# Two steps of a weight rounding and a one-row subtraction, moved from VectorE to GpSimd in a gated linear-attention and maxout-FFN kernel

## The chip, the cores and the metric

The kernel runs on one NeuronCore of a Trainium2 chip. The metric is the device time of one launch in microseconds (us). Three runs of the kernel before took 585.05, 585.9 and 587.58 us; the median is 585.9 us. Engine names in the profile: PE is TensorE (PEld its weight loads), DVE is VectorE, ACT is ScalarE, POOL is GpSimd, SP is SyncE, which issues the DMAs.

## The reference

Two stages are computed. The first is a recurrence over 768 steps, for 4 batches of 8 heads with head size 48. A complex gate turns and shrinks a state, and a real output is read from it:

```
mag = sqrt(a_re^2 + a_im^2);  scale = min(mag, 0.999) / (mag + 1e-6)
for t: S = (a_re + i a_im) * scale * S + k[t] v[t]^T      (complex S, real part read)
       y[t] = q[t] . Re(S)
```

The second is a feed-forward block on y, laid out as 3072 tokens by 384 features:

```
h = max(x @ w1, x @ w2, x @ w3)        # 384 -> 768
out = h @ w_out                        # 768 -> 384
```

The four weight matrices arrive as 64-bit floats, and the chip's matrix engine wants 32-bit ones. So the kernel turns each pair of 32-bit words into one float32 by work on bits: this is the part that the change touches.

## The kernel before, in words

**Tiling.** The tokens are cut into 12 groups (g = 0 to 11), each of 128 steps of two batches; the two batches of a group are called x and y. For each group the kernel loads a, k, q and v, works out the logarithm of the gate's size and its angle (the *turns*), sums them along the steps with matmuls, builds scaled and turned k and q, forms scores in blocks, carries a state from group to group, and puts the result through the feed-forward block. All float32.

**Order.** The order of the work is written out by hand. The string `SCHEDULE` is a list of steps (lines 21 to 130); `Wb0:0` is step b of weight block 0, `carry:1` the carry of group 1, `g0x:0` the first copy of scores of batch x in group 0. `program` walks the list once and each step issues its instructions. The class `Bound` (line 191) ties each instruction to the one before on the same engine, so that every engine executes its own instructions strictly in the order of the list. An engine that waits for one step holds up every later step of its own.

**Weights.** The four matrices make 12 blocks (`weight_blocks`, line 373), each 128 partitions by 768 float32 at the end. They are taken in the order 0, 3, 6, 9, 10, 11, 1, 2, 4, 5, 7, 8. Block i is loaded by `WLi` and then goes through `weight_step` (line 399):

- a (ACT): the absolute value of the upper word, read as a float, to the scratch `ex`;
- b (DVE before): limits to it, `max` with 2^-15 and `min` with `LAST`, one tensor_scalar, in place in `ex`;
- c (DVE): a shift of `ex` to the left by 3 bits;
- d (ACT): the lower word, scaled to a few bits, as a float in the block's own place `dst`;
- e (DVE before): the integer sum of `ex` and the bits of `dst`, in `ex`;
- f (DVE): the sign of the upper word joined to `ex`, into `dst`;
- g (DVE, some blocks): a difference of blocks, for the maximum.

b needs a, c needs b, e needs c and d, f needs e. The scratch `ex` lies in the tile `xhx`, which has two places for it; blocks take them in turn (`EX`, line 133), so that step a of a block needs step f of the block two before it. In the profile `ex` is named xhx, and `dst` is w or wo. The program gives step e on DVE to a custom instruction on 1536 halfwords, shown as CUSTOM_DVE_ANT_0 xhx<-w,xhx.

**The carry.** Step `carry` (line 538) subtracts from row 0 of the tile `ai` the turns that the group before ended with: one partition by 768 elements, for 10 of the 12 groups. Ahead of it ACT writes `ai` (`cpai`); behind it `addi` on DVE reads `ai`, or, in groups 0 and 1, the matmuls of `cs` do.

**GpSimd.** Before the change POOL has little to do: the constants of `constants_early` (line 278), the masks of `constants_late` (line 309, step `CL:0` of the list), which end with zeros in the two score tiles `atm`, and three memsets (`Z3`, `Z4`, `Z2`, line 928). The masks and the zeros are needed by `g0x:0` (line 722), a DVE copy of scores under the mask `maskd` into `atm`. Since the masks depend on nothing but POOL's own work, POOL makes them at 8.4 to 16.8 us, far ahead of `CL:0`'s place in the list.

Of the kernel before, what the change touches and what calls it, by code (L numbers as in the profile page):

```python
# [11 lines left out]
FP = mybir.dt.float32  # L12
U8 = mybir.dt.uint8
I32 = mybir.dt.int32
U32 = mybir.dt.uint32
AF = mybir.ActivationFunctionType
OP = mybir.AluOpType
# [119 lines left out]
def kernel(  # L137
# [36 lines left out]
    LAST = float(np.array(0x47EFFFFF, dtype=np.int32).view(np.float32))  # L174
# [13 lines left out]
    T = {}  # L188
# [18 lines left out]
    pe, dve, act, pool, sp = (Bound(e) for e in (nc.tensor, nc.vector, nc.scalar, nc.gpsimd, nc.sync))  # L207
    mm = pe.matmul

    def banks(nm, n=None):  # L210

        ps = psum.tile([P, 2, 512], FP, tag="ps", name=nm)
        T["ps"] = ps
        return ps if n is None else ps.rearrange("p a n -> p (a n)")[:, 0:n]
# [4 lines left out]
    def activation(func, **kw):  # L219

        need = SETS.get(func, T.get("set"))
        if need != T.get("set"):
            act.preload_act_table_set(need)
            T["set"] = need
        act.activation(func=func, **kw)

    def once(key, make):

        if key not in T:
            T[key] = make()  # L230
        return T[key]
# [167 lines left out]
    def weight_step(i, step):  # L399

        dst, src = blocks[i]
        n, m = dst.shape[1:]
        raw = T["raw", i].rearrange("p n (m w) -> p n m w", w=2)
        low, high = raw[:, :, :, 0].bitcast(U32), raw[:, :, :, 1]
        ex = xhx[:, 0:KD] if i in EX else xhx[:, KD + KF:]
        ex = ex.rearrange("p f t -> p (f t)").rearrange("p (n m) -> p n m", n=n).bitcast(I32)
        if step == "a":
            activation(out=ex.bitcast(FP), in_=high.bitcast(FP), func=AF.Abs)
        elif step == "b":
            dve.tensor_scalar(out=ex.bitcast(FP), in0=ex.bitcast(FP), scalar1=2.0 ** -15, scalar2=LAST,  # L410
                              op0=OP.max, op1=OP.min)
        elif step == "c":
            dve.tensor_single_scalar(out=ex, in_=ex, scalar=3, op=OP.logical_shift_left)
        elif step == "d":
            activation(out=dst, in_=low, func=AF.Copy, scale=2.0 ** -51, bias=2.0)
        elif step == "e":
            dve.tensor_tensor(out=ex, in0=ex, in1=dst.bitcast(I32), op=OP.add)
        elif step == "f":
            dve.scalar_tensor_tensor(out=dst.bitcast(I32), in0=high, scalar=-0x80000000, in1=ex,
                                     op0=OP.bitwise_and, op1=OP.bitwise_or)  # L420
        else:
            dve.tensor_tensor(out=dst, in0=dst, in1=blocks[i - i % 3][0], op=OP.subtract)
# [23 lines left out]
    def flat(t):  # L446
        return t.rearrange("p c h d -> p (c h d)")
# [22 lines left out]
    def gates(g, cs, name):  # L470

        if name not in names.split():
            return False
        lo, hi = cs[0] * DM, (cs[-1] + 1) * DM
        for nm in "Lwe":
            once((nm, g), lambda: nat1.tile([P, W], FP, tag=nm, name=nm))

        def part(nm):
            t = T[nm, g]
            return (flat(t) if len(t.shape) == 4 else t)[:, lo:hi]  # L480

        def flat_(nm):
            return T[nm, g]

        def of(t):
            return t.rearrange("p (c n) -> p c n", n=DM) if g < SUMS else t

        def total():
            return T["pw", g, lo][:, 0:len(cs), 0:DM] if g < SUMS else w

        L, w, e, ar, ai = (part(nm) if (nm, g) in T else None for nm in ("L", "w", "e", "ar", "ai"))
        if name == "sqr":
            activation(out=e, in_=ar, func=AF.Square)
        elif name == "sqi":
            activation(out=L, in_=ai, func=AF.Square)
        elif name == "add":
            dve._custom_dve(dve_ops.TENSOR_ADD_SAT, out=L, in0=L, in1=e, s0=LARGE, s1=SMALL)
        elif name == "lnL":
            activation(out=L, in_=L, func=AF.Ln)
        elif name == "expw":  # L500
            activation(out=w, in_=L, func=AF.Exp, scale=0.5)
        elif name == "expe":
            activation(out=e, in_=L, func=AF.Exp, scale=-0.5)
        elif name == "lne":
            activation(out=e, in_=e, func=AF.Ln, scale=1e-6, bias=1.0)
        elif name == "relu":
            activation(out=L, in_=L, func=AF.Relu, scale=-0.5, bias=lnmax)
        elif name == "Lnop":
            once(("Ln", g), lambda: nat2.tile([P, W], FP, tag="Ln", name="Ln"))
            dve.scalar_tensor_tensor(out=part("Ln"), in0=L, scalar=-LNMAX, in1=e, op0=OP.add, op1=OP.add)  # L510
        elif name == "abs":
            activation(out=e, in_=ar, func=AF.Abs)
        elif name == "pw":
            if g < SUMS:
                ps = T["pw", g, lo] = banks("pw")
                for n, c in enumerate(cs):
                    for i, t in enumerate(("w", "e")):
                        mm(out=ps[:, n, 0:DM], lhsT=ident, rhs=flat_(t)[:, c * DM:(c + 1) * DM], start=i == 0, stop=i == 1)
        elif name == "addw":
            if g >= SUMS:  # L520
                dve.tensor_tensor(out=w, in0=w, in1=e, op=OP.add)
        elif name == "lnw":
            activation(out=of(L), in_=total(), func=AF.Ln)
        elif name == "expL":
            activation(out=L, in_=L, func=AF.Exp, scale=-1.0)
        elif name == "mulai":
            dve.tensor_tensor(out=ai, in0=ai, in1=L, op=OP.mult)
        elif name == "mulw":
            dve.tensor_tensor(out=of(w), in0=total(), in1=of(L), op=OP.mult)
        elif name == "stt":  # L530
            dve.scalar_tensor_tensor(out=w, in0=w, scalar=2.0, in1=ai, op0=OP.subtract, op1=OP.mult)
        elif name == "sign":
            activation(out=ar, in_=ar, func=AF.Sign, bias=tiny)
        elif name == "cpai":
            activation(out=ai, in_=ar, func=AF.Copy, scale=-0.25, bias=0.25)
        elif name == "cpar":
            activation(out=ar, in_=ar, func=AF.Copy, scale=-1.0 / math.pi)
        elif name == "carry":
            if g % NS > 0:
                dve.tensor_tensor(out=ai[0:1], in0=ai[0:1], in1=T["carry", g], op=OP.subtract)  # L540
        elif name == "atan":
            activation(out=w, in_=w, func=AF.Arctan)
        elif name == "mulr":
            dve.tensor_tensor(out=w, in0=w, in1=ar, op=OP.mult)
        elif name == "addi":
            if g >= SUMS:
                dve.tensor_tensor(out=w, in0=w, in1=ai, op=OP.add)
        return True
# [372 lines left out]
    def run(name, g):  # L921
# [12 lines left out]
        elif name[0] in "TtMm" and name[1:].isdigit():  # L934
            product(name[0], int(name[1:]))
        elif name[0] == "W":
            i = int(name[2:])
            weight_load(i) if name[1] == "L" else weight_step(i, name[1])
        elif name[0] in "Uu" and name[1:].isdigit():
            up(g, int(name[1]), int(name[2]), name[0])  # L940
        elif name[0] in "Uu" and name[1:3].isdigit():
            up_one(2 * g + "xy".index(name[3]), int(name[1]), int(name[2]), name[0])
        elif name in SEVEN or name in ("ox", "oy") and g > 0:
            seven(g, name)
        elif name[0] == "J":
            join(name[1])
        elif name[-1] in "01" and gates(g, [int(name[-1])], name[:-1]):
            pass
        elif gates(g, list(range(C)), name):
            pass  # L950
        else:
            c = "xy".index(name[-1])
            x, name = g * C + c, name[:-1]
            if name in ("Lr", "Li"):
                load_a(g, c, *(("ar", a_re) if name == "Lr" else ("ai", a_im)))
            elif name in ("Lk", "Lq"):
                load_kq(g, c, *(("k", k) if name == "Lk" else ("q", q)))
            elif name == "Lv":
                load_v(g, c)
            else:  # L960
                assert angles(g, c, name) or turns(g, c, name) or factors(x, name) or scores(x, name) \
                    or state(x, name) or outputs(x, name) or project(x, name), name
# [45 lines left out]
```

## Time and profile before

| what | value |
|---|---|
| median of three runs | 585.9 us (585.05 to 587.58) |
| span of the profiled execution, first to last instruction | 585.0 us |
| mean granted TensorE clock | 0.980 |
| PE busy | 537.6 us, 92% of the span |
| DVE busy | 506.0 us, 86% |
| ACT busy | 439.4 us, 75% |
| POOL busy | 15.5 us, 3% |

A row of the profile by groups reads: engine, operation, what is written <- what is read, shapes, x count | busy us, mean ns of one | idle time of the engine just before. A row of the timeline reads: start in us from the span's start, duration in us, engine, line, operation; in brackets, the engine's idle time ahead of it and what ended it. Nearly all instructions carry line 200, the recording helper in `Bound`, so they are told apart by operation and tile. Two DVE instructions that follow each other overlap by about 0.08 us: the 128x768 ones last 0.95 us, and start 0.87 us apart when nothing holds them; the 128x768 tensor_scalars last 0.56 us and take a slot of 0.47 us.

### The profile page before, as it was taken

The page shows a single profiled execution, that of the slowest core. Times are in us where ns is not written, and L with a number is a line of the kernel's source. Part 1 is how long each engine was busy: PE and PEld are TensorE (multiplying, and loading weights), DVE is VectorE, ACT ScalarE, POOL GpSimd, SP SyncE. Part 2 cuts the span into 40 slices and gives each one's busy share as a digit, 9 for nine tenths or more (in the row PEclk, how much of TensorE's full clock was granted, in tenths as well). Part 3 has the DMA queues.
Part 4 walks back from the last instruction along what each step waited for, and adds up shares of the span by engine and source line. Part 5 has one row for each costly group of instructions (what it writes and reads, how often), then busy time and mean ns, then how long its engine had stood idle before and what let it go on. Part 6 is the DMA issues. An engine that isn't in the chain of part 4 may idle for free.

```text
span 585.0 us, 22777 instructions
## 1 busy us (share of the span) xinstructions
PE 537.6 (92%) x10118; PEld 454.6 (78%) x10118; DVE 506.0 (86%) x784; ACT 439.4 (75%) x740; POOL 15.5 (3%) x50
## 2 busy tenths in 40 slices
PE   2649979898999999999999999999999999999897
PEld 0336668767888888888898888898887888888886
DVE  5999999979898999999889889989998999877504
ACT  7999999857788778788788987887896797643110
POOL 8100100000000000000000000000000000000000
PEclk9778999989999999999999999999999999999999
DMA  8984134414204214223223233143043031010000
GB/s 269 251 181 109 56 85 76 90 33 80 43 18 107 46 35 93 43 48 80 43 53 76 41 62 75 33 97 60 14 97 70 7 73 37 3 43 2 30 0 27
DMA packets 136544, 39.24 MB, mean 67 GB/s; under 512 B 129152, under 2 KB 132224, under 8 KB 136448
## 3 DMA queue, kind: packets, MB, share of 16 engines
q1 hardware_dynamic: 136448, 37.80, 29.2%
q8 instruction: 79, 1.29, 0.9%
q14 instruction: 17, 0.14, 0.1%
HBM read 33.03 MB, written 4.72 MB: 65 GB/s over the span
## 4 chain that ended last, share of the span: by engine, by line
PE 82%; ACT 11%; issue 3%; DMA 1%; DVE 1%; SPq 1%; DVEq 0%; ACTq 0%
PE up L200 31%; PE op L200 22%; PE y L200 6%; PE A L200 5%; PE tp L200 4%; PE dk L200 4%; PE sums L200 3%; PE cs L200 2%; PE wm L200 2%; ACT xhx L200 2%; PE B L200 1%; PE F L200 1%; ACT w L200 1%; ACT e L200 1%; ACT L200 1%
## 5 line engine op out<-in xcount | busy, mean ns | idle before, releaser
L200 PE MATMUL up<-xhx,w 128*128 128x256 f32 x792 | 176.5, 382 | 0.9 <-ACT xhx L200 0.6
L200 PEld LDWEIGHTS up<-xhx,w 128*128 128x128 f32 x792 | 148.7, 190 | 21.6 <-ACT xhx L200 1.1
L200 DVE TENSOR_TENSOR Q<-Q,f 112x512 f32<-112x512 f32 (+2 forms) x72 | 68.3, 952 | 9.4 <-ACT Q L200 9.4
L200 ACT ACT_TABLE_LOAD x48 | 61.6, 1283 | 1.6 <-PEq L992 0.8
L200 PE MATMUL op<-wo,xhx 128*128 128x192 f32 (+1 forms) x220 | 47.4, 363 | 0.0
L200 DVE TENSOR_TENSOR xhx<-xhx,up 128x768 f32<-128x768 f32 x22 | 20.9, 952 | 26.8 <-PE up L200 26.8
L200 PEld LDWEIGHTS op<-wo,xhx 128*128 128x128 f32 x220 | 37.0, 190 | 6.6 <-issue 0.3
L200 PE MATMUL y<-atm,vb 128*32 128x64 f32 x1152 | 39.0, 221 | 2.1 <-issue 2.1
L200 ACT ACTIVATE f<-F 48x280 f32<-48x280 f32 x96 | 38.4, 400 | 3.5 <-DVE g L200 2.3
L200 DVE TENSOR_TENSOR ot<-ot,op 128x192 f32<-128x192 f32 (+1 forms) x66 | 26.7, 418 | 15.7 <-ACT ot L200 12.0
L200 PE MATMUL y<-QG,g 112*32 112x64 f32 x1408 | 38.4, 219 | 0.0
L200 ACT COPY atm<-B 32x128 f32<-32x128 f32 x96 | 24.6, 256 | 18.2 <-DVE atm L200 12.9
L200 PE MATMUL A<-Q,K 112*32 112x80 f32 x1536 | 33.2, 234 | 5.5 <-issue 5.5
L200 ACT COPY ot<-op 128x192 f32<-128x192 f32 (+1 forms) x13 | 4.5, 344 | 44.2 <-PE op L200 44.2
L200 PEld LDWEIGHTS y<-atm,vb 128*32 128x32 f32 x1152 | 32.4, 109 | 6.4 <-issue 3.4
L200 PEld LDWEIGHTS A<-Q,K 112*32 112x32 f32 x1536 | 28.0, 110 | 10.4 <-issue 9.1
L200 PEld LDWEIGHTS y<-QG,g 112*32 112x32 f32 x1408 | 34.9, 109 | 1.3 <-issue 1.2
L200 PE MATMUL op<-wo,strassen 128*128 128x192 f32 x176 | 33.5, 332 | 0.3 <-issue 0.3
L200 DVE COPY_PREDICATED atm<-masko,A 128x256 f32<-128x256 uint8 x72 | 31.1, 432 | 1.1
L200 ACT COPY Q<-tp 112x1024 f32<-112x1024 f32 x24 | 24.4, 1019 | 8.7 <-PE tp L200 8.7
L200 PEld LDWEIGHTS op<-wo,strassen 128*128 128x128 f32 x176 | 28.6, 190 | 3.0 <-issue 2.1
L200 PE MATMUL op<-w,strassen 128*128 128x192 f32 x176 | 30.7, 327 | 0.0
(145 smaller groups left out, 1144.0 us busy)
## 6 DMA issues: line engine op xcount, KB each, us to landing
ar<-in_a_re_dram SPq DMA_DIRECT2D x24, 192.0 KB
ai<-in_a_im_dram SPq DMA_DIRECT2D x24, 192.0 KB
q<-in_q_dram SPq DMA_DIRECT2D x96, 48.0 KB
vb<-in_v_dram SPq DMA_DIRECT2D x96, 48.0 KB
k<-in_k_dram SPq DMA_DIRECT2D x96, 48.0 KB
out_dram<-ot SPq DMA_DIRECT2D x24, 192.0 KB
w<-in_moe_w_dram SPq DMA_DIRECT2D x3, 768.0 KB
xhx<-in_moe_w_dram SPq DMA_DIRECT2D x3, 768.0 KB
```

Source lines behind the costliest of these rows:

```text
L200: ins = f(*a, **kw)
```

## The change

Three calls go from `dve` to `pool`. The step list is the same.

```diff
         elif step == "b":
-            dve.tensor_scalar(out=ex.bitcast(FP), in0=ex.bitcast(FP), scalar1=2.0 ** -15, scalar2=LAST,
+            pool.tensor_scalar(out=ex.bitcast(FP), in0=ex.bitcast(FP), scalar1=2.0 ** -15, scalar2=LAST,
                               op0=OP.max, op1=OP.min)
...
         elif step == "e":
-            dve.tensor_tensor(out=ex, in0=ex, in1=dst.bitcast(I32), op=OP.add)
+            pool.tensor_tensor(out=ex, in0=ex, in1=dst.bitcast(I32), op=OP.add)
...
         elif name == "carry":
             if g % NS > 0:
-                dve.tensor_tensor(out=ai[0:1], in0=ai[0:1], in1=T["carry", g], op=OP.subtract)
+                pool.tensor_tensor(out=ai[0:1], in0=ai[0:1], in1=T["carry", g], op=OP.subtract)
```

In the built program 34 instructions leave DVE's queue and join POOL's: 12 of step b, 12 of step e, 10 carries. The queues of PE, ACT and SP are unchanged. On POOL the new order is: the early constants; b0, e0, b3, e3, b6, b9, e6, e9, b10, e10, b11, e11, b1, e1, b2, b4, e2, e4; then the masks of `CL:0` and the zeros of `atm`; then b5, the three memsets, the carry of group 1, e5, b7, e7, b8, the carry of group 2, e8, and the other eight carries. Step e on POOL is one 128x768 int32 tensor_tensor in place of the custom instruction.

## Prediction

> **What bounds the kernel now.** I read the busy time by stage first, since the moved weight steps all lie in the first 100 us (step a of the first block starts at 10.49, step f of the last ends at 97.64). The columns are start:end, length, then PE, PEld, DVE, ACT, POOL busy.
>
> ```profile
> core 0: us, PE busy (x) PEld busy (x) DVE busy (x) ACT busy (x) POOL busy (x), PEclk, DMA share, GB/s
> 10.00:55.00 45.00, 28.51 (x264) 17.41 (x264) 42.18 (x63) 44.55 (x74) 6.27 (x13) 0.77 0.82 206
> 55.00:100.00 45.00, 40.24 (x768) 32.12 (x767) 42.82 (x66) 43.34 (x73) 1.64 (x3) 1.00 0.34 76
> 100.00:500.00 400.00, 389.74 (x7897) 335.23 (x7899) 368.35 (x561) 321.79 (x536) 0.00 (x0) 1.00 0.28 57
> ```
>
> From 10 to 100 us ACT is the bound (44.55 and 43.34 of 45 us), and DVE is close behind it (42.18 and 42.82, so 2.8 and 2.2 us idle). From 100 to 500 us PE is the bound (389.74 of 400), and DVE has 31.7 us idle. The chain of waits agrees: from 10 to 48 us it is made of ACT pieces, and from about 100 us mostly of PE pieces. Hence DVE time taken off before 100 us is worth little by itself, for ACT is as full, and what makes DVE late there makes ACT late soon, and in the end PE.
>
> **What the change removes.** The groups by shape:
>
> ```profile
> L200 DVE TENSOR_TENSOR ai<-ai,carry 1x768 f32<-1x768 f32 x10 | 9.4, 939 | 0.0
> L200 DVE CUSTOM_DVE_ANT_0 xhx<-w,xhx 128x1536 uint16<-128x1536 uint16 x9 | 8.6, 953 | 0.3
> ...
> L200 DVE TENSOR_SCALAR xhx<-xhx 128x768 f32<-128x768 f32 x12 | 6.7, 557 | 1.6 <-ACT xhx L200 1.4
> ```
>
> In slots (start to start) b is 0.47 us, e and a carry 0.87 us each. A block frees 1.34 us of DVE, the 12 blocks 16.1 us, the 10 carries 8.7 us: 24.8 us in all, of which 17.8 us lie before 100 us (two carries are there).
>
> **What it adds on POOL.** No row shows such an operation on POOL, so each is bounded by POOL's own groups:
>
> ```profile
> L200 POOL TENSOR_SCALAR_AFFINE_SELECT KB<-KB 128x128 f32<-128x128 f32 x2 | 0.8, 402 | 0.1
> ...
> L200 POOL COPY mid<-mid 64x64 f32<-64x64 f32 x1 | 0.2, 233 | 0.1
> ...
> L200 POOL COPY cuts<-cuts 64x35 f32<-64x35 f32 x1 | 0.2, 208 | 0.1
> ```
>
> *b* has one input. From COPY with 35 and 64 elements (208 and 233 ns) the slope is 25/29 = 0.86 ns an element and the fixed part 0.18 us, which gives 0.18 + 768 x 0.86 ns = 0.84 us. *e* and the carries have two inputs. The low end is the same 0.84 us. A second read at the same slope gives 1.50 us; the step of the affine select from 64 elements (0.29 us, undisturbed at 10.95) to 128 (0.402) is 1.75 ns an element, which gives 0.29 + 704 x 1.75 ns = 1.52 us. The high end is the 402 ns row taken as cost per element (3.1 ns): 2.4 us. I take 0.84 and 1.5 us, the row of the same kind and two rows that meet. The Trainium skill (GPSIMD Engine Reference, section "Performance versus the Vector engine") has a two-input add of 2048 elements at 4497 ns there against 2293 on VectorE; scaled, an estimate of 1.69 us for 768. By it the forecast would be some 3 us later.
>
> **Beside DVE, or in its way?** The trace shows this at 7 to 16 us, where POOL makes masks beside DVE:
>
> ```profile
> 10.95 0.29 POOL L200 TENSOR_SCALAR_AFFINE_SELECT KB<-KB 128x64 f32<-128x64 f32 x1
> ```
> ```profile
> 12.99 0.84 POOL L200 TENSOR_SCALAR_AFFINE_SELECT KB<-KB 128x64 f32<-128x64 f32 x1
> ```
> ```profile
> 12.75 0.97 DVE L200 CUSTOM_DVE_ANT_0 xhx<-w,xhx 128x1536 uint16<-128x1536 uint16 x1
> ```
> ```profile
> 14.57 0.90 POOL L200 CAST masko<-KB 64x96 uint8<-64x96 f32 x1
> ```
> ```profile
> 13.85 0.56 DVE L200 TENSOR_SCALAR xhx<-xhx 128x768 f32<-128x768 f32 x1
> 14.33 1.02 DVE L200 SCALAR_TENSOR_TENSOR w<-w,xhx 128x768 int32<-128x768 int32 x1
> ```
>
> The same select takes 0.29 us alone and 0.84 beside a two-input DVE instruction, and ends at 13.83, 0.11 us after DVE's 13.72. The CAST at 14.57 ends at 15.47, 0.13 us after DVE's 15.34. So POOL waits until DVE's instruction is over. The other way round, the DVE row at 14.33 lasts 1.02 us where its kind lasts 0.95: POOL, which had waited since 13.89, went first when the tensor_scalar ended at 14.41, and DVE stood still for the 0.07 us of POOL's 96 elements. Neither starves, and they take turns. With 768 elements instead of 96 I read the same rule as a hold of 0.66 us for b (0.84 less the fixed part) and 1.32 us for e and a carry. That DVE stands still for so long is worked out and not seen. The Trainium skill says the same of these two engines (SBUF — State Buffer, section "Who interferes with whom"): a VectorE instruction with two SBUF inputs, or in a 2-port mode, and a GpSimd instruction that reads SBUF exclude each other for a whole instruction. The rows above agree for short GpSimd instructions.
>
> **The sum.**
>
> *Blocks 0 to 4 in the list's order (9 blocks, 10 to 55 us).* Per block DVE loses 1.34 us of slots and gets holds of 0.66 + 1.32 = 1.98 us: +0.64 us. To it come the places where DVE waits for POOL outright. I followed the first block: a0 ends at 11.38; b0 11.42 to 12.26; c0 to 12.86 (12.60 before); e0 12.91 to 14.41 (13.72 before). Behind e0 on POOL stands b3, which takes its turn at once and holds until 15.25, so f0 runs 15.25 to 16.2 where it ended at 15.34. Step a6 on ACT needs f0's scratch and starts at 15.45, only 0.11 us after it, so ACT too is late by some 0.75 us. With the same turns e3 goes 17.1 to 18.5 behind `Lnop1`, b6 holds to 19.3, and f3 ends at 20.25 (18.56 before): +1.7. Per block some 0.8 us; for nine blocks +6.7 us on DVE.
>
> *The masks.* Before, they ran at 8.4 to 16.8 us. Now they stand behind e4, which ended at 50.40 on DVE, 5.43 us ahead of `g0x:0` at 55.83. The masks and the first zeros of `atm` take 5.2 us undisturbed (0.41 + 0.87 + 0.5 + 0.26 + 2.1 + 0.55 + 0.52), but five two-input DVE instructions lie in that stretch and each makes one mask wait. I put the end 2 us after `g0x:0` could start, and DVE waits there with everything behind it: +2 us (0 to 4).
>
> *Blocks 5, 7, 8 and the carries of groups 1 and 2 (55 to 100 us).* Slots lost 3 x 1.34 + 2 x 0.87 = 5.8 us, holds 3 x 1.98 + 2 x 1.32 = 8.6 us: +2.8 us. Here b and e have 3 to 10 us until they are needed, so nothing waits outright, except that the carry of group 1 stands behind memsets that end at 66.48 (it ended at 66.72 before). DVE has 2.2 us idle, so I take +2.
>
> *Eight later carries.* Each costs DVE 1.32 - 0.87 = 0.45 us, but on POOL it may run when `cpai` ends, 2 us ahead of its old place, and the step behind that place waits for PE in seven of the eight groups, as here:
>
> ```profile
> 322.03 0.94 DVE L200 TENSOR_TENSOR ai<-ai,carry 1x768 f32<-1x768 f32 x1
> 324.43 0.95 DVE L200 TENSOR_TENSOR xhx<-xhx,up 128x768 f32<-128x768 f32 x1 [1.46 <-PE up L200]
> ```
>
> So the saved slot becomes a longer wait for PE, and the hold is eaten by it: 0 (-1 to +4).
>
> DVE: 6.7 + 2 + 2 = 10.7 us late at 100 us. Of this some 0.7 us is eaten by DVE's own idle time (4.7 us of 10 to 100 us; what PE does later, in a fixed order, gives nothing back). So +10 on the profiled execution's 585.0 us, which is 595.0. The median lies 0.9 us above that span: **596 us**.
>
> The ends: with 0.84 us for all, a block costs 1.32 of holds for 1.34 of slots, and only the masks' +1 remains: 587. With 2.4 us for e and the carries, the 12 blocks cost 0.9 us more each and the two early carries too, +12.6, the masks +2, and the later carries +4: 615.
>
> **Rivals.**
>
> *R1, the holds don't come about* (POOL's 768 elements let DVE through). Then DVE is freed of 17.8 us before 100 us, but f0 still comes late by about 0.7 us, since e0 ends at 14.41 whoever is let through, and ACT has only 0.45 + 1.66 us idle in those 90 us. The masks still cost up to 1. Time 585 to 588. Against it: the DVE row of 1.02 us.
>
> *R2, faster.* As R1, and DVE's lead makes all block steps early, so that ACT's 2.1 us of idle time and some 2 us of the DVE pieces on the chain (at 129.7 to 134.5 us) go: 585.9 - 4 = 582. It decides if POOL's e is under about 1 us and holds nothing. For it: DVE is 94% busy there. Against it: a6 started 0.11 us behind f0, so any longer e is felt at once.
>
> *R3, dear integers.* Step e adds 32-bit integers on POOL, of which no row tells. At 4 us each, twelve holds of 2.5 us more: +30 over my forecast, 626. Nothing in the trace excludes it; the CASTs, which convert types, are not dear apart from their waits.
>
> *R4, nothing moves:* excluded, since the built program has the 34 instructions on POOL.
>
> **Chances.** Forecast (588.9 to 615): 0.79. R1: 0.11. R2: 0.04. R3 (over 615): 0.06. What a measurement here can tell from no change is about 0.5%, 2.9 us, so the same is 583.0 to 588.8. R1 is all the same: 0.11; R2 faster: 0.04; forecast and R3 slower: 0.85. The range for 8 in 10 takes in both ends of the unknown price: 587 to 615.
>
> **What would show it.** In the profile after: POOL TENSOR_SCALAR of 128x768 at about 0.84 us when undisturbed and TENSOR_TENSOR at about 1.5, both longer where DVE is at work; DVE rows of 0.95 us stretched up to 2.2 beside them; ACT's a6 at about 16.2 instead of 15.45; the mask memset of 128x384 at 55 to 58 instead of 8.40, and `g0x:0` with idle time that POOL ends; the first `up` matmuls some 10 us later, and the stretch from 100 to 500 us of the old length. I am wrong if DVE's rows keep their lengths (R1, R2), if POOL's e is 3 us or more (R3), or if ACT starts to fall back only at the masks.

## The result and the profile after

The changed kernel takes 606.38 us (median of three runs, 605.19 to 607.07) against 585.9 us before: slower by 20.5 us between the medians, and by a ratio of 1.0333 with a 95% interval of 1.0299 to 1.0368, which is 17.5 to 21.6 us. The span of its profiled execution is 604.4 us, 19.4 us more than before. It is slower, along the path that was forecast (DVE late before 100 us, then ACT, then PE), and by twice the forecast 10 us.

POOL's groups by shape show the largest surprise at once:

```profile
L200 POOL TENSOR_SCALAR xhx<-xhx 128x768 f32<-128x768 f32 x12 | 37.0, 3082 | 10.5 <-ACT xhx L200 10.4
L200 POOL TENSOR_TENSOR ai<-ai,carry 1x768 f32<-1x768 f32 x10 | 22.6, 2264 | 375.7 <-ACT ai L200 375.7
L200 POOL TENSOR_TENSOR xhx<-xhx,w 128x768 int32<-128x768 int32 x9 | 18.9, 2101 | 14.3 <-DVE xhx L200 13.5 <-ACT L L200 0.7
```

A step b lasts 3.08 us on average, where DVE took 0.56 and the forecast had 0.84. The two-input forms, at 2.1 to 2.3 us, are nearer to the forecast's 1.5 us and the waits it put on top. The busy time by stage (columns as before: PE, PEld, DVE, ACT, POOL):

```profile
core 0: us, PE busy (x) PEld busy (x) DVE busy (x) ACT busy (x) POOL busy (x), PEclk, DMA share, GB/s
...
10.00:55.00 45.00, 20.06 (x136) 11.79 (x136) 32.73 (x35) 35.60 (x58) 37.73 (x15) 0.65 0.75 187
55.00:100.00 45.00, 34.25 (x591) 23.59 (x590) 36.06 (x44) 35.37 (x58) 26.66 (x26) 0.89 0.29 74
```

From 10 to 55 us POOL is now the fullest engine (37.73 of 45 us). ACT, which was full with 44.55, waits 9.4 us. DVE has more idle time, and its busy time contains standstills. The timeline of DVE in the first blocks shows both kinds of loss (start, duration, instruction, idle time ahead of it and what ended it):

```profile
16.27 1.57 DVE L200 SCALAR_TENSOR_TENSOR w<-w,xhx 128x768 int32<-128x768 int32 x1 [1.99 <-POOL xhx L200]
19.01 0.56 DVE L200 TENSOR_SCALAR xhx<-xhx 128x768 int32<-128x768 int32 x1 [1.17 <-POOL xhx L200]
19.48 0.55 DVE L200 SCALAR_TENSOR_TENSOR Ln<-L,e 128x384 f32<-128x384 f32 x1
21.74 1.57 DVE L200 SCALAR_TENSOR_TENSOR w<-w,xhx 128x768 int32<-128x768 int32 x1 [1.70 <-POOL xhx L200]
...
27.21 2.15 DVE L200 TENSOR_SCALAR xhx<-xhx 128x768 int32<-128x768 int32 x1 [0.51 <-POOL xhx L200]
```

The brackets are waits for POOL's result. The durations are holds: step f lasts 1.57 us beside a b on POOL instead of 0.95, and a step c lasts 2.15 instead of 0.56 beside an e. On ACT the step a6, which the forecast singled out, follows. Its row before, and after:

```profile
15.45 0.90 ACT L200 ACTIVATE xhx<-wo 128x768 f32<-128x768 f32 x1
```
```profile
17.87 0.89 ACT L200 ACTIVATE xhx<-wo 128x768 f32<-128x768 f32 x1 [2.94 <-DVE w L200]
```

It starts at 17.87 us instead of 15.45. Before the first masked copy of scores DVE waits for the zeros that end the masks (before, and after):

```profile
55.83 0.72 DVE L200 COPY_PREDICATED atm<-maskd,A 128x512 f32<-128x512 uint8 x1
```
```profile
71.75 0.73 DVE L200 COPY_PREDICATED atm<-maskd,A 128x512 f32<-128x512 uint8 x1 [2.45 <-POOL atm L200]
```

So that copy is 15.9 us later. PE then gets what it needs late:

```profile
76.59 1.10 PE L200 MATMUL tp<-ident,uq 64*112 64x64 f32 x16 [6.02 <-DVE uq L200]
77.62 6.24 PE L200 MATMUL wm<-wo,uk 128*128 128x384 f32 x12
...
86.62 0.55 PE L200 MATMUL cs<-ai,upto 128*64 128x192 f32 x4 [1.78 <-POOL ai L200]
```

The last row waits for the carry of group 1, which runs on POOL from 84.77 to 86.56 us, behind the memsets, and the second of these had waited 8.20 us, until the `wm` matmuls ended. In the kernel before the same row stood at 67.51 and had waited 1.00 us, for ACT.

The first `up` matmul (the first product of the feed-forward block) stands at 95.64 us against 75.96 (+19.7), the last ends at 589.92 against 570.52 (+19.4). So the whole loss arises ahead of the PE-bound stage, and nothing is won or lost in it.

### The profile page after: what moved, and what is told of

Read it like the earlier page. It is cut to its first block, busy times and chain, and to the rows that moved or that the text cites. A ratio compares the mean times of both kernels' runs of the same rounds, so it can differ in the third digit from the quotient of the medians.

```text
span 604.4 us, 22830 instructions
## 1 busy us (share of the span) xinstructions
PE 540.4 (89%) x10118; PEld 455.8 (75%) x10118; DVE 504.7 (84%) x750; ACT 441.0 (73%) x740; POOL 98.8 (16%) x84
## 4 chain that ended last, share of the span: by engine, by line
PE 78%; POOL 6%; issue 5%; ACT 4%; DVE 3%; DMA 1%; SPq 1%; DVEq 0%; POOLq 0%
PE up L200 30%; PE op L200 22%; PE y L200 7%; POOL xhx L200 5%; PE A L200 5%; PE tp L200 4%; PE dk L200 4%; PE cs L200 3%; PE sums L200 3%; PE F L200 2%; PE B L200 1%; DVE w L200 1%; DMA vb<-in_v_dram 1%; ACT L L200 1%; DMA ar<-in_a_re_dram 1%
## 5 line engine op out<-in xcount | busy, mean ns | idle before, releaser
L200 POOL TENSOR_TENSOR ai<-ai,carry 1x768 f32<-1x768 f32 x10 | 22.6, 2264 | 375.7 <-ACT ai L200 375.7
L200 DVE TENSOR_TENSOR Q<-Q,f 112x512 f32<-112x512 f32 (+2 forms) x72 | 70.4, 982 | 9.2 <-ACT Q L200 9.2
L200 POOL TENSOR_SCALAR xhx<-xhx 128x768 f32<-128x768 f32 x12 | 37.0, 3082 | 10.5 <-ACT xhx L200 10.4
```

Source lines behind the costliest of these rows:

```text
L200: ins = f(*a, **kw)
```

## The experiments

Each run was timed beside the kernel before on the same chip, whose medians lay between 585.55 and 587.54 us. The differences in us are between medians; the ratios, worked out from the single runs, put some of them otherwise by up to 1.6 us. Three theories were set against each other: **length** (a b lasts long on POOL, and every block waits for it), **holds** (DVE stands still beside POOL), and **masks** (their new place in POOL's queue).

### One part at a time

```diff
 e1  -dve.tensor_scalar(out=ex...    +pool.tensor_scalar(out=ex...      (step b alone)
 e2  -dve.tensor_tensor(out=ex...    +pool.tensor_tensor(out=ex...      (step e alone)
 e3  -dve.tensor_tensor(out=ai[0:1]  +pool.tensor_tensor(out=ai[0:1]    (the carries alone)
```

Step b alone:

> Step b alone on POOL, steps e and the carries on DVE as before. Theory 1 (length: a b takes 2.77 us on POOL, undisturbed too, where DVE took 0.56 and I assumed 0.84, and every block waits for that): most of the change's loss is here, +8 to +13 us over the kernel before. Theory 2 (holds: DVE stands still beside POOL, and its rows before 200 us are stretched by 20 us in all): a b stretches a DVE row by only 0.62 us and frees a slot of 0.47, so twelve of them give 1.8 us and the wait for the masks 2 more: +3 to +5 us. Theory 3 (the masks' place in POOL's queue is the main loss): +7 us or more here and in the run with e alone.

Step e alone:

> Step e alone on POOL, steps b and the carries on DVE as before. An e lasts 1.80 us on POOL and stretches the DVE row beside it by about 1.6 us, for a freed slot of 0.87. Theory 1 (length of b): +3 to +6 us. Theory 2 (holds): twelve times 0.75 us and the wait for the masks, +8 to +12 us. Theory 3 (masks' place): +7 us or more, and DVE waits for POOL at the first masked copy for over 5 us.

The carries alone:

> The ten carries alone on POOL. All theories: within 1.5 us of the kernel before. In the changed kernel a carry lasts 1.8 to 2.5 us on POOL and stretches a DVE row by 0.43 us in the eight later groups, for a freed slot of 0.87 us that DVE spends waiting for PE. If the carries matter after all, the stretch from 100 to 500 us is longer by over 2 us.

| part on POOL | median, us | before beside it | ratio (95% interval) |
|---|---|---|---|
| b | 596.57 | 585.55 | 1.0184 (1.0161 to 1.0208) |
| e | 590.97 | 585.55 | 1.0084 (1.0058 to 1.0110) |
| carries | 587.79 | 585.55 | 1.0039 (1.0022 to 1.0056) |

Step b costs +11.0 us, within what length expected and far over the +3 to +5 of holds. Step e costs +5.4, inside the +3 to +6 that the length theory left for it and under the +8 of holds. The carries' +2.2 us is a little more than any theory gave; in their trace PE waits 2.19 us for POOL ahead of the `cs` matmuls of group 1, where it had waited 1.00 us for ACT. The three make 18.7 of the 20.5 us. The masks are not the main loss: in the run with e alone DVE waits 1.89 us for them, and that run is only +5.4 in all.

### The prices by themselves

```diff
     program(SCHEDULE, 0)
+    for n in (96, 384, 768):
+        b_form(A[:, 0:n], A[:, 0:n])        # max and min, as step b
+    b_form(lo, lo, one=True)                # max alone
+    b_form(lo, lo, ops=(OP.mult, OP.add))
+    b_form(lo, lo, one=True, ops=(OP.mult,))
+    pool.tensor_copy(out=hi, in_=lo)
...
+    for form in ("b", "e"):                 # beside eight two-input DVE instructions
...
```

> The kernel before with a series of POOL instructions added behind its work, on a scratch tile, and twice a POOL instruction beside eight two-input DVE instructions of 256 elements; its total time says nothing. Theory 1: the limits (max and min, 768 elements) last 2.77 us here too, and the cost lies in the operation: by the element, about 3.4 ns, so 0.5 us at 96 and 1.5 us at 384. If the two operations of one instruction are what makes it dear, max alone lasts about half; if it is max and min as such, multiply and add stay at about 0.85 us like a copy. The two-input forms: 1.80 us, integers no dearer. Beside DVE: a b holds one DVE row by 0.62 us, a two-input form holds one by about 1.6 us (theory 2 needs this; if DVE's rows of 256 elements pass in between, the hold is not for the whole instruction).

The timeline of POOL in this kernel, one execution: max and min at 96, 384 and 768 elements, then max alone, multiply and add, a copy, and the integer sum at 768:

```profile
583.19 0.53 POOL L200 TENSOR_SCALAR strassen<-strassen 128x96 f32<-128x96 f32 x1 [517.19 <-DMA out_dram<-ot]
```
```profile
583.80 1.49 POOL L200 TENSOR_SCALAR strassen<-strassen 128x384 f32<-128x384 f32 x1
```
```profile
585.37 2.77 POOL L200 TENSOR_SCALAR strassen<-strassen 128x768 f32<-128x768 f32 x1
```
```profile
591.07 2.13 POOL L200 TENSOR_SCALAR strassen<-strassen 128x768 f32<-128x768 f32 x1
```
```profile
593.28 0.83 POOL L200 TENSOR_SCALAR strassen<-strassen 128x768 f32<-128x768 f32 x1
```
```profile
596.39 0.82 POOL L200 COPY strassen<-strassen 128x768 f32<-128x768 f32 x1
```
```profile
603.38 1.80 POOL L200 TENSOR_TENSOR strassen<-strassen 128x768 int32<-128x768 int32 x1
```

The limits cost 2.77 us with nothing beside them, 3.33 ns an element between 384 and 768 (1.487 and 2.767 us). Max alone takes 2.13 us (the row at 591.07), multiply and add in one instruction 0.83 (at 593.28), a multiply alone again 2.13, and a copy 0.82 us (at 596.39), which is what the forecast had taken for b. So neither the second operation nor max and min as such is the cause: of the one-input forms tried, only multiply-and-add and the copy run at 1.1 ns an element. Why is not shown. Integers are no dearer than floats: 1.80 us both, and a carry of one partition takes 1.79. The Trainium skill (GPSIMD Engine Reference, section "When to use GPSIMD") says that one-input work there "is roughly line-rate". The copy agrees (0.82 us, where a two-input row of 768 elements takes 0.95 on DVE); the limits don't (2.77 us, where DVE took 0.56 for the same step), and here the measurement decides.

Beside DVE the two forms differ. Of eight two-input DVE rows of 256 elements (0.43 us each) one is held beside the b, and 0.93 us long; the next four start and pass at their usual length while the b goes on:

```profile
606.20 0.93 DVE L200 TENSOR_TENSOR xhx<-xhx 128x256 f32<-128x256 f32 x1
```
```profile
607.16 0.43 DVE L200 TENSOR_TENSOR xhx<-xhx 128x256 f32<-128x256 f32 x1
```

Beside the two-input form one DVE row lasts until after POOL's end:

```profile
610.38 1.91 DVE L200 TENSOR_TENSOR xhx<-xhx 128x256 f32<-128x256 f32 x1
```

The b (605.85 to 608.81) holds DVE for 0.5 us of its 2.96; the two-input form (610.02 to 612.00) holds until it ends.

### The change with a cheap b, and with one in between

The test of the length theory: the same kernel, queue and waits, with a b of 0.83 us (e5), and one of 2.13 us (e10).

```diff
 e5
-            pool.tensor_scalar(... scalar1=2.0 ** -15, scalar2=LAST, op0=OP.max, op1=OP.min)
+            pool.tensor_scalar(... scalar1=1.0, scalar2=0.0, op0=OP.mult, op1=OP.add)
 e10
+            pool.tensor_single_scalar(... scalar=2.0 ** -15, op=OP.max)
```

> The changed kernel, but step b on POOL multiplies by 1 and adds 0 instead of setting limits (it leaves the limits out): the same place and queue, and by the added instruction series 0.83 us instead of 2.77. Theory 1 (length of b): the loss falls from 20 us to my forecast's own +10, 593 to 598 us. Theory 2 (holds, which stay: 0.62 us for b, 1.6 for e): the loss stays at +15 us or more, over 601 us.

> The changed kernel, but step b on POOL takes the lower limit alone (it leaves the upper limit out), which by the series lasts 2.13 us, between 0.83 (multiply and add: +12 us over the kernel before) and 2.77 (both limits: +20.5). If the loss goes with the length of b, it lies on the line between: 12 + 8.5 x (2.13 - 0.83) / (2.77 - 0.83) = +17.7 us, 1.5 either way. If it goes with max and min as such, or with the second operation, it is +20 or +12.

e5 takes 598.73 us beside 586.9, ratio 1.0228 (1.0192 to 1.0264): +11.8 us. e10 takes 605.23 beside 587.54, ratio 1.0314 (1.0279 to 1.0349): +17.7 us, on the line.

```profile
L200 POOL TENSOR_SCALAR xhx<-xhx 128x768 f32<-128x768 f32 x12 | 29.7, 2472 | 12.0 <-ACT xhx L200 11.9
```

This is the b of e10, 2.47 us on average beside DVE; that of e5 lasts 1.17 on average. So with b at 0.83, 2.13 and 2.77 us undisturbed the loss is 11.8, 17.7 and 20.5 us: it goes with the length of b, by about 4.5 us for each microsecond. By the ratios the three losses are 13.4, 18.4 and 19.5 us, each 2 us either way, and by the first `up` in the traces 9.6, 16.8 and 19.7; so the direction is sure and the slope is only known to lie at 3 to 5. DVE's waits for POOL shrink alongside: 16.8 us in the changed kernel, 15.2 in e10, 12.4 in e5. With b at the assumed price the loss is +11.8 us (+11.3 to +15.5 by the ratio), near the forecast's 10 or a little over. (e5 lies 0.7 us above the window that length had given, and below that of holds.)

The same cheap b without e and the carries:

> Step b alone on POOL, as multiply and add (it leaves the limits out), steps e and the carries on DVE. The same step with its limits was +11 us. Length theory: 0.83 us against 0.56 on DVE and a hold of 0.62 for a slot of 0.47 leave +1 to +3 us, a part of it the wait for the masks. If it stays over +6 us, what costs is that b is on another engine at all.

590.2 us beside 587.54, ratio 1.0051 (1.0029 to 1.0074): +2.7 us, where b with its limits cost +11.0. So most of what b costs is how long it takes there, and not that it is on another engine. In what is left, DVE waits 2.22 us for the masks.

### Holds without anything that waits

```diff
             dve.scalar_tensor_tensor(...)          # step f
+            if i in (0, 3, 6, 9, 10, 11, 1):
...
+                pool.tensor_tensor(out=scratch, in0=dst, in1=dst, op=OP.subtract)
```

> The kernel before, with seven more POOL subtractions of 128x768 (two inputs), one behind each step f of the first seven blocks, whose result nobody uses or waits for; the masks come behind them, at about 43 us, well ahead of their use. Nothing but the hold is added. If a held DVE row costs what it is late (1.1 to 1.7 us a time, seven times 1.4 is 10 us, less some 2 us of DVE's idle time), the loss is +6 to +9 us, and the loss of the run with e alone (+5.4, where each e also frees 0.87 us) is then made of holds. If holds don't reach the end and only a late result does, it is +2 us or less.

592.86 us beside 586.15, ratio 1.0131 (1.0096 to 1.0166): +6.7 us, as expected. The rows of DVE and of POOL at the fifth of them:

```profile
35.58 1.82 DVE L200 TENSOR_TENSOR w<-w,ar 128x384 f32<-128x384 f32 x1
```
```profile
35.32 1.66 POOL L200 TENSOR_TENSOR vb<-wo 128x768 f32<-128x768 f32 x1 [3.69 <-issue]
```

A DVE row of 0.55 us lasts 1.82 and ends 0.41 us after POOL's. By the timeline seven DVE rows are longer by 8.2 us in all, though no step waits for these subtractions. One thing more is in this run: the masks, behind the seventh subtraction, come at 50.7 to 63.7 us and not well ahead of their use, and DVE waits 1.04 us for them at the masked copy. So the hold of DVE by a two-input POOL instruction is real, and costs some 0.8 to 1 us each at the end. How the +5.4 of the run with e alone divides into holds, less the freed slots, and waits for POOL (3.6 us in its trace, 1.89 of them for the masks) stays open. Holds was wrong as the main cause of the surplus, and right as a mechanism: the forecast's basis stands.

### The masks first, the late blocks, the late carries

```diff
 e6  the run with e alone, and CL:0 moved to the head of the step list
 e7  -dve.   +(pool if i in (5, 7, 8) else dve).     (steps b and e)
 e8  -dve.   +(pool if g > 2 else dve).              (the carry)
```

> As the run with e alone on POOL, but the masks stand first in the list, so POOL makes them ahead of the first e. If DVE's wait of 1.89 us for POOL at the first masked copy was the masks' whole part, the time falls by 1 to 2 us, to +3.5 to +4.5 us over the kernel before; theory 3 (masks the main part) has it at +1 us or less. The rest is the e itself: longer by 0.85 us, with DVE held.

> Steps b and e on POOL for the blocks 5, 7 and 8 alone, where what needs them comes 3 to 10 us later; the masks stay early. Theory 1 (length, felt only where a step is waited for): within 1 us of the kernel before. Theory 2 (holds): three times 0.15 + 0.75 us, +2 to +3 us.

> The carries of the eight later groups alone on POOL (those of groups 1 and 2 on DVE). The run with all ten was +2.2 us. If that comes from the two early carries (behind memsets, before matmuls that wait), this is within 0.7 us of the kernel before; if it comes from the later ones beside PE, it is +1.5 to +2.5 us.

e6: 592.61 beside 586.9, ratio 1.0101 (1.0085 to 1.0118), no better than e alone (1.0084). The expected gain did not come: the masked copy has no wait for POOL any more, but stands at 61.69 us as in e2 (61.70), since the masks now hold up the first e (15.14 instead of 12.28 us). The work was moved from one wait into another, so this run doesn't price the masks by themselves.

e7: 586.35 beside 586.9, ratio 0.9994 (0.9980 to 1.0008): the same as before, as length had it. Where the result is needed late, a 3 us b on POOL costs nothing, and the 4.0 us of DVE slots it frees bring nothing either.

e8: 587.28 beside 586.9, ratio 1.0005 (0.9982 to 1.0028): the later carries cost nothing. The rest of the +2.2 us of e3 would then lie with the two early ones, one of which makes PE wait; with intervals of 0.2% this is likely and not certain.

No run beats the kernel before.

## Why the prediction was right in its path, and short by half

**Right: what bounds, and the sign.** Time added before 100 us comes out at the end in full (+19.7 at the first `up`, +19.4 at the last), and the PE-bound stage keeps its length. One reading was too broad: the chain of the kernel before does not run on ACT from 10 to 100 us, but on PE from 48.3 to 66.6, with two stretches of `wm` in it.

**Wrong, the mis-sized term: "I take 0.84" for b.** Measured: 2.77 us undisturbed, 3.08 on average. The slope came from COPY rows, and a copy does take 0.82 us at 768 elements; but step b is no copy. The forecast bounded e from above by the affine select's cost per element (2.4 us) and gave b no upper bound. Setting b to 0.83 us takes 8.7 of the 20.5 us away (e5; 6.1 by the ratios). So the result lies inside the range by luck: the range's end at 615 was made of an e at 2.4 us and +4 for the later carries, and neither came. The slip per block was put at 0.8 us; step f of block 4 starts at 64.92 instead of 51.19, +13.7 over nine blocks, 1.5 each. a6 starts 2.4 us late instead of 0.75.

**Nearly right: e and the carries at 1.5 us.** Measured 1.80 us undisturbed. That two ways of working it out met at 1.5 was luck in part: the slope of 1.75 ns took the 128x128 select at 0.402 us, and the same trace has another of that shape that is no longer than the 128x64 one:

```profile
7.22 0.29 POOL L200 TENSOR_SCALAR_AFFINE_SELECT upto<-upto 128x128 f32<-128x128 f32 x1
```

The estimate of 1.69 us, from the Trainium skill (GPSIMD Engine Reference, section "Performance versus the Vector engine"), was closer.

**Right for e, half right for b: the holds.** For two inputs DVE waits until POOL ends (e4, e9). For b the hold is 0.5 to 0.62 us, close to the assumed 0.66, but by luck: it was worked out as the whole of a short instruction, and is a fraction of a long one. The Trainium skill's rule (SBUF — State Buffer, section "Who interferes with whom") has the whole instruction shut out the other engine; the two-input rows agree, the b rows don't.

**Wrong in part: "Neither starves, and they take turns".** In the run with b alone a mask instruction is kept waiting through five DVE rows without a gap and takes 5 us (below).

**Right: the masks, +2 us.** DVE waits 2.45 us there (2.84 and 1.89 in e1 and e2). That the end feels it in full isn't shown, since e6 only moved it.

**Stage 55 to 100 us, +2.** From the masked copy (+15.9) to the first `up` (+19.7) it is +3.8. Of that, 2.1 us is one run of twelve `wm` matmuls, 6.24 us instead of 4.14, of which PE spent the first 4.28 us at a granted clock of 0.50 and the rest at 1.00; the forecast had no term for it. Some 0.8 us more is PE's wait for the early carry, 1.78 us instead of the 1.00 for ACT. The forecast had seen that this carry stands behind the memsets, and priced it at nothing, because the memsets ended in time before; the second of them waits for `wm`, and so came late with it.

**Right: the eight later carries, 0** (e8, and the unchanged PE-bound stage).

**The rivals.** R1 and R2 fell, since DVE's rows are stretched. R3, dear integers, fell too: integers cost what floats cost. The dear operation was the one that the forecast held to be cheap.

## What to carry to other kernels

Before giving a step to an engine that has not run it, time that very operation there, at its size and form: a copy says nothing of a pair of limits. Count the added length along each chain that needs the step, not the busy time it frees; where nothing needed it soon (e7) 3 us cost nothing, and in a tight chain each microsecond on twelve steps cost 3 to 5. And a two-input POOL instruction takes DVE's time as well as its own, so moving such a step saved DVE nothing here where DVE was at work.

## What the runs showed of the hardware that was not expected

The length of a one-input POOL instruction of 128x768 depends on its form: 0.82 us for a copy, 0.83 for multiply and add, 2.13 for one operation with a constant (max or multiply), 2.77 for max and min. The longer forms leave DVE free for most of their length: a DVE row beside one is 0.62 us longer, whether the form lasts 2.77 us (step f, 1.57 us instead of 0.95) or 2.13 (the same row in e10).

POOL can starve. POOL, then DVE, in the run with b alone:

```profile
54.13 5.00 POOL L200 TENSOR_SCALAR_AFFINE_SELECT KB<-KB 128x128 f32<-128x128 f32 x1
```
```profile
54.45 0.95 DVE L200 CUSTOM_DVE_ANT_0 xhx<-w,xhx 128x1536 uint16<-128x1536 uint16 x1
55.32 0.95 DVE L200 SCALAR_TENSOR_TENSOR w<-xhx 128x768 int32<-128x768 int32 x1
56.19 0.95 DVE L200 SCALAR_TENSOR_TENSOR w<-strassen,xhx 128x768 int32<-128x768 int32 x1
57.06 1.82 DVE L200 TENSOR_TENSOR w<-w,w 128x768 f32<-128x768 f32 x2
58.80 0.95 DVE L200 TENSOR_TENSOR w<-pw,L 128x768 f32<-128x768 f32 x1
```

An instruction that took 0.40 us in the kernel before takes 5.00. Five DVE rows with two inputs in SBUF follow each other with no gap, and it ends at 59.13, after the sixth has started, one that reads PSUM (`pw`). In the changed kernel the same instruction got its turn between two such rows. In e9 a select took 4.91 us and in e11 a cast 4.84, through the same five DVE rows; both ended about 0.1 us after the fifth. What decides was not tested.

The granted TensorE clock was 0.50 from 75.1 to 81.9 us in the changed kernel. It fell 4.5 us into an idle stretch of PE (70.57 to 76.59), and stayed there for 5.3 us of work. In the kernel before, where PE has no such stretch at that point, it was 1.00 from 49.5 us to 117.7. That the idle stretch is the cause isn't shown.
